# Local attention scores: from VectorE products to TensorE strips that pass through DRAM

## The chip, the core and the metric

The program runs on one core of a Trainium2 chip. The core has a matrix engine (TensorE, PE in the profile, with its weight loads shown apart as PEld), VectorE (DVE), ScalarE (ACT), GpSimd (POOL), and SyncE (SP), whose only work here is to issue DMAs. The engines run side by side, each takes its own instructions strictly in order, and they wait for each other by semaphores. The metric is the device time of one execution in microseconds; lower is better.

## The reference

Eight batches, eight heads, 576 positions, 64 values per head. Two attentions are added, and the sum goes through a maxout layer and an output layer:

```
q_d, k_d, v_d = mean of 4 neighbouring positions (576 -> 144)
out_up    = repeat(softmax(q_d k_d^T / 8) v_d, 4)          # pooled attention
mask      = |row - column| < 4                             # 7 keys per row
out_local = softmax(where(mask, q k^T / 8, -1e9)) v        # local attention
x = (out_up + out_local) as [4608 tokens, 512]
h = max(x w1, x w2, x w3)                                  # 512 -> 768, three times
y = h w_out                                                # 768 -> 512
```

All inputs are float32 (the weights arrive as 64-bit floats and are split on the device). Local attention needs, for each position, seven scores, those of the keys from three before it to three after it.

## The kernel before

**Blocks and groups.** The tokens are cut into nine blocks of 512: block j (0 to 7) holds the first 512 positions of batch j, and block 8 the last 64 positions of all batches. A group n is half a block's heads: block j has the groups 2j and 2j+1, of four heads each (`HH`). For every block, attention makes `x`, `transposes` turns it into the high and low halves `xhi` and `xlo` (a float32 product is made of three fast ones), `mlp_in` runs 216 matmuls of 128x128 by 512 columns, and `mlp_out` 72 more. In the profile these are the lines `pm<-xhi_0r,whi_0r` and so on, and `pm<-wo_1r,hh_0r`; "MLP matmul" below means one of them.

**Dense groups.** The groups 0 to 3 (`DENSE`) do local attention on TensorE: `band_load` loads q and k with positions on partitions (in pieces of 256 B), `band_transposes` turns them with 16 TensorE transposes and ACT copies (plus two small ones for the halo), `band_scores` makes 128x134 strips of scores, whose useful part is a band of seven, and `band_values` multiplies the softmaxed strips with v.

**Sparse groups.** The groups 4 to 17 make their seven scores on VectorE. In `scores(n)`, each of the four heads has q with four neighbouring positions per partition and k with a halo; one multiplication gives `prod` (7 offsets x 256 values per partition), and one reduction gives `s` (28 scores). The softmax runs on `s` for the four heads at once. `values(n)` multiplies v by the seven probabilities, one instruction group per offset, on ACT (four instructions) or POOL (one), and adds them up on DVE into `x`.

**Pooled attention.** `halves` adds neighbours of q, k and v (tiles `hqk`, `qd`, `kd`, `hv`, `vd`), TensorE transposes the pooled q and k into `qkT`, and `tail_pooled` does the last 16 pooled rows apart (tiles `traw`, `th`, `tq`, two more TensorE transposes). `pooled_scores` and `pooled_values` then work on `qkT` (tiles `pd`, `pdt`, `ptl`, `ptd`, `pt`, `ptt`).

**PSUM.** Two sets of four banks: `pm` for the MLP and `pa` for attention.

**What sets the order.** No engine order is written by hand. A `Recorder` records every operation with a priority, the engines that may run it, and the buffers it needs; `place` then goes through the operations as a list scheduler with a table of assumed durations (`price`), chooses engine and buffer, and fixes each engine's order before the program is built. An operation of which two engines are capable goes to the one that would end first. All instructions are issued from one line (L348 before the change, L374 after), so the profile's groups are told apart by their tile names, not by lines. Tiles that share a buffer carry the buffer's name: `pv` also holds the dense groups' q and k, `whi` and `wlo` the dense groups' strips, `y` and `wo` parts of the dense groups' values.

The heart of `scores(n)` before:

```
prod = new([P, NO, FAC * D], tag="prod", name=f"prod_{n}_{g}")
dve.tensor_tensor(out=prod, in0=window(kt, 0, NO), in1=qt.unsqueeze(1).broadcast_to([P, NO, FAC * D]), op=ALU.mult)
dve.tensor_reduce(out=s[:, g], in_=prod.rearrange("p o (f d) -> p o f d", d=D), axis=AX.X, op=ALU.add)
```

Of the kernel before, what the change touches and what calls it, by code (L numbers as in the profile page):

```python
# [10 lines left out]
F32 = mybir.dt.float32  # L11
# [22 lines left out]
SEG = FAC * P  # L34
DENSE = (0, 1, 2, 3)
# [4 lines left out]
def shape_constants():  # L40
    ident = np.eye(P, dtype=np.float32)
    o = np.arange(NO)[:, None] - 3
    f = np.arange(FAC)[None, :]
    mask = np.full((2, P, NO, FAC), 3.0e38, np.float32)
    mask[0, 0][(f + o) < 0] = -8.0e9
    mask[1, TAIL - 1 :: TAIL][:, (f + o) >= FAC] = -8.0e9
    diag = (np.arange(HH * TAIL)[:, None] // TAIL == np.arange(HH)[None, :]).astype(np.float32)
    mask = np.ascontiguousarray(np.stack([mask[0][:, :3], mask[1][:, 4:]])).reshape(2, P, 3 * FAC)
# [3 lines left out]
    return ident, mask, diag, np.ascontiguousarray(band.astype(np.float32))  # L52


ENGINES = ("PE", "DVE", "ACT", "POOL", "SP")
DONE_NS = {"PE": 230.0, "DVE": 150.0, "ACT": 190.0, "POOL": 200.0}
BIAS = {"PE": 0.0, "DVE": 0.0, "ACT": 0.0, "POOL": 0.0}
# [19 lines left out]
class Recorder:  # L77
# [6 lines left out]
    def __init__(self, nc, tc, sb, psum):  # L84
        self.nc, self.tc, self.pools = nc, tc, {"SB": sb, "PSUM": psum}
# [5 lines left out]
    def tile(self, shape, dtype, tag=None, bufs=1, name=None, space="SB"):  # L91
# [6 lines left out]
        info = {"tag": key, "k": len(order[1]), "acc": [], "ops": [], "psum": space == "PSUM", "name": name, "words": int(np.prod(shape[1:])), "dtype": dtype}  # L98
# [4 lines left out]
    def region(self, ap):  # L103
        info = self.of.get(ap.tensor.name)
        if info is None:
            return None
        dims = [tuple(d) for d in list(ap.ap)]
# [14 lines left out]
    def add(self, forms):  # L122

        o = Op()
        o.forms = forms
# [37 lines left out]
    def price(self, eng, method, args, kw):  # L163
# [7 lines left out]
        if eng == "PE":  # L171
            if method == "transpose":
                return max(75.0, 0.86 * n), False
            if args[1].dtype == F32R:
                return 231.0, False
            return 2.0 * max(64.0, 0.86 * n), False
# [20 lines left out]
    def place(self):  # L197
# [43 lines left out]
        while len(out) < len(ops):  # L241
# [17 lines left out]
            if len(o.forms) > 1:  # L259
                ends = []  # L260
                for a in o.forms:
                    c, lock = o.cost[a]
                    ends.append((max(free[a], o.ready, port if lock else 0.0) + c + BIAS[a], a))
# [9 lines left out]
            if e == "SP":  # L273
# [3 lines left out]
                ap = next(a for a in (o.forms[e][0][1][:2]) if a.tensor.name in self.of)  # L277
                other = next(a for a in (o.forms[e][0][1][:2]) if a.tensor.name not in self.of)
                size = list(ap.ap)[0][1] * elems(ap) * 4
                rate = 330.0 if list(other.ap)[-1][1] >= 256 else 180.0  # L280
# [41 lines left out]
    def emit(self):  # L322
# [5 lines left out]
        def real(a):  # L328
# [5 lines left out]
            slot = (space, tag, info["slot"], kind)  # L334
            if slot not in store:
# [24 lines left out]
def local_global_attention_maxout_kernel(ctx: ExitStack, tc: tile.TileContext, q, k, v, w1, w2, w3, w_out, ident_d, mask_d, diag_d, band_d, out):  # L360
# [3 lines left out]
    rec = Recorder(nc, tc, sb, psm)  # L364
# [29 lines left out]
    mask = new([P, 2, 3 * FAC], name="mask")  # L394
# [5 lines left out]
    KW = SEG + 6  # L400
    KB = 2 * FAC * (P + 6)
    band = [new([P, 2 * KW + 2 * (P + 6)], tag=f"w{x}{NFT - 1}", name=f"bandqk_{x}") for x in ("hi", "lo")]
    bandmask = band[0][:, 2 * KW :].rearrange("p (u x) -> p u x", u=2)
# [34 lines left out]
    def load_constants():  # L438
# [3 lines left out]
        sp.dma_start(mask, mask_d.rearrange("m p x -> p m x"))  # L442
        sp.dma_start(diag, diag_d)
        sp.dma_start(bandmask, band_d)
        for pr in range(2):
            dve.memset(band[pr][:, SEG : SEG + 3], 0.0)
# [41 lines left out]

    def tail_pooled(n):
        j, h0 = n // 2, HH * (n % 2)  # L490
        st = state[n]
        tq = st["tq"] = new([N64, 2, 2, D], tag="tq", name=f"tq_{n}")
        for g, src in enumerate((q, k, v)):
            raw = new([N64, FAC * D], tag="traw", name=f"traw_{n}_{g}")
            sp.dma_start(raw, dram(src, ((j * H + h0) * S + FAC * P) * D, [[S * D, HH], [FAC * D, TAIL], [1, FAC * D]]))
            h = new([N64, 2 * D], tag="th", name=f"th_{n}_{g}")
            halves(n, "t", raw, h)
            if g < 2:
                tt(tq[:, g], h[:, :D].unsqueeze(1).broadcast_to([N64, 2, D]), h[:, D:].unsqueeze(1).broadcast_to([N64, 2, D]), ALU.add)
            else:  # L500
                vt = st["vt"] = new([N64, HH, D], tag="vt", name=f"vt_{n}", bufs=2)
                vs = new([N64, D], tag="vs", name=f"vs_{n}")
                tt(vs, h[:, :D], h[:, D:], ALU.add)
                tt(vt, vs.unsqueeze(1).broadcast_to([N64, HH, D]), diag.unsqueeze(2).broadcast_to([N64, HH, D]), ALU.mult)

    def pooled_scores(n):
        st = state[n]
        tq, qkT = st["tq"], st["qkT"]
        qt = qtail[n % 2]
        pst = bank([P, 2, 2, 2, TAIL], "pa", f"pstail_{n}")  # L510
        for i in range(2):
            pe.transpose(pst[:, i], tq[:, i], ident[:N64, :N64])
        for i in range(2):
            pp = slice(64 * i, 64 * i + 64)
            act.copy(qt[pp, :, i], pst[pp, 0, :, i])
            act.copy(qkT[pp, 1, :, P:], pst[pp, 1, :, i])
# [64 lines left out]
    def scores(n):  # L581
        j, h0 = n // 2, HH * (n % 2)
        st = state.setdefault(n, {})
        s = st["p"] = new([P, HH, NO, FAC], tag="s", bufs=2, name=f"s_{n}")
        if j < B:
            hs = {w: new([P, HH, 2 * D], tag="hqk", bufs=2, name=f"h{w}_{n}") for w in "qk"}
            ds = {w: new([P, HH, D], tag=f"{w}d", name=f"{w}d_{n}") for w in "qk"}
        for g in range(HH):
            h = h0 + g
            qt = new([P, FAC * D], tag="q", bufs=2, name=f"q_{n}_{g}")  # L590
            kt = new([P, HW], tag="k", bufs=2, name=f"k_{n}_{g}")
# [5 lines left out]
            if j < B:  # L597
                halves(n, "q", qt, hs["q"][:, g])
                halves(n, "k", kt[:, 3 * D : 7 * D], hs["k"][:, g])
        if j < B:  # L600
            for w in "qk":
                tt(ds[w], hs[w][:, :, :D], hs[w][:, :, D:], ALU.add)
        e0 = 0 if j < B else 4 * FAC
        sf = s.rearrange("p g o f -> p g (o f)")[:, :, e0 : e0 + 3 * FAC]
        dve.tensor_tensor(out=sf, in0=sf, in1=mask[:, j // B].unsqueeze(1).broadcast_to([P, HH, 3 * FAC]), op=ALU.min)
        mx = new([P, HH, FAC], tag="mx", bufs=2, name=f"mx_{n}")
        dve.tensor_reduce(out=mx, in_=s.rearrange("p g o f -> p g f o"), axis=AX.X, op=ALU.max)
        dve.tensor_tensor(out=s, in0=s, in1=mx.unsqueeze(2).broadcast_to([P, HH, NO, FAC]), op=ALU.subtract)
        act.activation(s, s, AF.Exp, scale=0.125)
        z = new([P, HH, FAC], tag="z", bufs=2, name=f"z_{n}")  # L610
        dve.tensor_reduce(out=z, in_=s.rearrange("p g o f -> p g f o"), axis=AX.X, op=ALU.add)
        dve.tensor_scalar_add(z, z, EPS)
        dve.reciprocal(z, z)
        dve.tensor_tensor(out=s, in0=s, in1=z.unsqueeze(2).broadcast_to([P, HH, NO, FAC]), op=ALU.mult)
        if j < B:
            qkT = st["qkT"] = new([P, 2, 2, SD], tag="qkT", name=f"qkT_{n}")
            ps = bank([P, 2, 2, P], "pa", f"psqk_{n}")
            for i, w in enumerate("qk"):
                for pr in range(2):
                    pe.transpose(ps[:, i, pr], ds[w][:, 2 * pr : 2 * pr + 2, :], ident)  # L620
            copy(qkT[:, :, :, :P], ps)

    def values(n):
# [7 lines left out]
        for g in range(HH):  # L631
# [6 lines left out]
            for o in range(NO):  # L638
                muls = [("activation", (pv[:, o, f], vv[:, (o + f) * D : (o + f + 1) * D], AF.Copy), dict(scale=p[:, g, o, f : f + 1])) for f in range(FAC)]
                kw = dict(out=pv[:, o : o + 1], in0=window(vv, o, 1).rearrange("p o (f d) -> p o f d", d=D), in1=p[:, g, o : o + 1].unsqueeze(3).broadcast_to([P, 1, FAC, D]), op=ALU.mult)  # L640
                rec.add({"ACT": muls, "POOL": [("tensor_tensor", (), kw)]})
# [11 lines left out]
    def band_load(n):  # L653
        j, h0 = n // 2, HH * (n % 2)
        st = state.setdefault(n, {})
        q4 = st["q4"] = new([P, FAC, HH, D], tag="pv", bufs=2, name=f"q4_{n}")
        k4 = st["k4"] = new([P, FAC, HH, D], tag="pv", bufs=2, name=f"k4_{n}")
        kh = st["kh"] = new([3, HH, D], tag="qd", name=f"kh_{n}")
        base = (j * H + h0) * S * D
        for t, src in ((q4, q), (k4, k)):  # L660
            for u in range(FAC):
# [242 lines left out]
```

## Time and profile before

| | |
|---|---|
| runs (three) | 861.69, 864.99, 870.87 us; median 864.99 us |
| profiled execution, first to last instruction | 867.8 us |
| busy: PE, PEld, DVE, ACT, POOL | 92%, 71%, 84%, 53%, 31% of that span |
| granted TensorE clock, mean | 0.945 |

The profiled execution's time is known as its span alone; it lies between the second and the third run, 2.8 us above the median. A busy PE is not a PE at its peak, because matmuls overlap and their ends are modelled: whether PE could take more is read from the distance between the starts of matmuls, and from a stretch in which nothing else runs. Idle time of an engine that is not the bottleneck costs nothing.

### The profile page before, as it was taken

What the parts mean: (1) busy time and instruction counts of PE and PEld (TensorE: products, weight loads), DVE (VectorE), ACT (ScalarE), POOL (GpSimd) and SP (SyncE); (2) the same over time, 40 slices, a digit from 0 to 9 for tenths busy, and PEclk for the clock granted to TensorE, in tenths of its full rate; (3) what the DMA queues carried; (4) which work ended last, traced back from release to release, by engine and by line L of the source; (5) the groups of instructions that cost most, each with busy time, mean ns of one, the idle gap of its engine ahead of it and who ended that gap; (6) DMA issues with size and microseconds to landing.
All of it is one profiled execution on the core that took longest, in us unless ns stands there. A gap on an engine that the chain in (4) does not pass through costs nothing.

```text
span 867.8 us, 12330 instructions
## 1 busy us (share of the span) xinstructions
PE 794.8 (92%) x3992; PEld 612.3 (71%) x3992; DVE 727.2 (84%) x1201; ACT 461.5 (53%) x1607; POOL 269.3 (31%) x345
## 2 busy tenths in 40 slices
PE   3779996898999999998989899988999999999997
PEld 3557775686777777676767677766777777788885
DVE  3889959699999999999999999999999999851220
ACT  3656646442738484756466564557564848721111
POOL 0011200003346364334354444444443623500000
PEclk9555998689999999999999999999999999999999
DMA  6844304233323323332223221432232233101002
GB/s 182 228 123 132 95 21 143 77 110 116 100 74 97 116 81 96 100 97 81 88 86 119 88 83 59 158 92 76 80 125 77 74 106 115 35 1 49 1 1 48
DMA packets 71675, 78.71 MB, mean 91 GB/s; under 512 B 30108, under 2 KB 51930, under 8 KB 71610
## 3 DMA queue, kind: packets, MB, share of 16 engines
q1 hardware_dynamic: 71610, 77.93, 29.5%
q8 instruction: 31, 0.51, 0.2%
q14 instruction: 34, 0.28, 0.1%
HBM read 68.47 MB, written 9.44 MB: 90 GB/s over the span
## 4 chain that ended last, share of the span: by engine, by line
DVE 53%; PE 30%; issue 8%; ACT 6%; DMA 1%; SPq 1%; POOL 1%; DVEq 0%; ACTq 0%; POOLq 0%
PE pm L348 23%; DVE pv L348 9%; DVE prod L348 8%; DVE s L348 7%; DVE t L348 7%; PE pa L348 6%; ACT pv L348 4%; DVE wo L348 3%; DVE xlo_0r L348 2%; DVE nm L348 2%; DVE hh_0r L348 1%; DVE x L348 1%; DVE mxb L348 1%; DVE hh_1r L348 1%; DMA v<-in_v_dram 1%
## 5 line engine op out<-in xcount | busy, mean ns | idle before, releaser
L348 PE MATMUL pm<-xlo_0r,whi_0r 128*128 128x512 f32 x648 | 259.7, 401 | 0.0
L348 PE MATMUL pm<-xhi_0r,whi_0r 128*128 128x512 f32 x648 | 259.1, 401 | 0.0
L348 PE MATMUL pm<-xhi_0r,wlo_0r 128*128 128x512 f32 x648 | 258.6, 399 | 0.0
L348 ACT ACTIVATE pv<-v,s 128x64 f32<-128x64 f32 x840 | 210.7, 340 | 28.6 <-DVE s L348 16.7
L348 POOL TENSOR_TENSOR pv<-v,s 128x256 f32<-128x256 f32 x182 | 140.1, 799 | 148.4 <-DVE x L348 64.3
L348 PEld LDWEIGHTS pm<-xhi_0r,wlo_0r 128*128 128x128 f32 x648 | 123.3, 190 | 27.9 <-issue 0.9
L348 PEld LDWEIGHTS pm<-xhi_0r,whi_0r 128*128 128x128 f32 x648 | 123.2, 190 | 28.0 <-issue 0.7
L348 PEld LDWEIGHTS pm<-xlo_0r,whi_0r 128*128 128x128 f32 x648 | 123.1, 190 | 28.0 <-issue 0.7
L348 DVE TENSOR_TENSOR t<-pm,t 128x512 f32<-128x512 f32 x108 | 73.7, 683 | 71.8 <-PE pm L348 70.9
L348 DVE TENSOR_TENSOR prod<-k,q 128x1792 f32<-128x1792 f32 x56 | 117.5, 2098 | 0.2
L348 DVE TENSOR_REDUCE s<-prod 128x28 f32<-128x1792 f32 x56 | 112.4, 2007 | 0.5
L348 DVE TENSOR_TENSOR pv<-pv 128x768 f32<-128x768 f32 x112 | 102.5, 915 | 2.1
L348 PE MATMUL pm<-wo_1r,hh_0r 128*128 128x512 f32 x216 | 87.2, 405 | 4.0 <-ACT wo_1r L348 2.4
L348 PE MATMUL pm<-wo_1r,hh_1r 128*128 128x512 f32 x216 | 86.8, 404 | 0.1
L348 ACT COPY y<-pm 128x512 f32<-128x512 f32 x43 | 24.9, 585 | 57.9 <-PE pm L348 57.4
L348 ACT CAST hh_0r<-t 128x512 fp32r<-128x512 f32 x30 | 18.6, 618 | 67.6 <-DVE t L348 67.6
L348 PEld LDWEIGHTS pm<-wo_1r,hh_0r 128*128 128x128 f32 x216 | 41.1, 190 | 15.0 <-ACT wo_1r L348 3.1
L348 POOL TENSOR_TENSOR th<-traw 64x128 f32<-64x128 f32 x26 | 24.1, 927 | 82.4 <-DMA traw<-in_k_dram 36.2
L348 ACT COPY t<-pm 128x512 f32<-128x512 f32 x54 | 31.3, 581 | 32.8 <-PE pm L348 32.6
L348 PEld LDWEIGHTS pm<-wo_1r,hh_1r 128*128 128x128 f32 x216 | 41.0, 190 | 10.1 <-ACT hh_1r L348 0.5
L348 PE MATMUL pm<-wo_0r,hh_0r 128*128 128x512 f32 x120 | 46.0, 394 | 0.0
L348 PE MATMUL pm<-wo_0r,hh_1r 128*128 128x512 f32 x96 | 38.5, 402 | 0.0
(184 smaller groups left out, 1088.5 us busy)
## 6 DMA issues: line engine op xcount, KB each, us to landing
v<-in_v_dram SPq DMA_DIRECT2D x55, 320.0 KB
k<-in_k_dram SPq DMA_DIRECT2D x55, 320.0 KB
out_dram<-y SPq DMA_DIRECT2D x36, 256.0 KB
q<-in_q_dram SPq DMA_DIRECT2D x56, 128.0 KB
hh<-in_moe_w_dram SPq DMA_DIRECT2D x12, 512.0 KB
pv<-in_moe_w_dram SPq DMA_DIRECT2D x6, 512.0 KB
pv<-in_moe_w_out_dram SPq DMA_DIRECT2D x6, 512.0 KB
pv<-in_q_dram SPq DMA_DIRECT2D x16, 128.0 KB
```

The source lines that it names most:

```text
L348: getattr(self.engines[o.eng], method)(*map(real, args), **{k: real(x) for k, x in kw.items()})
```

## The change

The sparse groups' scores move to TensorE, and all groups get q and k already transposed.

- The program's inputs become `qt` and `kt` (two heads x 64 values on partitions, positions along the row; `kt` padded by three positions on each side), with `qe` and `ke` for block 8. They are prepared outside the device program. `load_qk(n)` loads two tiles of q and two of k per group with rows of 2304 to 2328 B; `band_transposes`, the loads of the halo and the loads of pooled tails of q and k are gone.
- `scores(n)` makes, for each pair of heads, 16 matmuls of 64 positions by 70 keys (strips in which seven of 70 are useful) into two `pa` banks, copies the banks to `sm`, writes `sm` to a DRAM buffer `scr` (four DMAs of 64 x 8 pieces of 280 B per group), and reads it back with a row pitch one element longer, so that the diagonal band lands as seven neighbours (one DMA of 2048 pieces of 28 B per group). The softmax on `s` is as before, with its axes in another order.
- `pooled_qk(n)` adds neighbours directly on the transposed tiles (`hp`, then `qkT`), so that the pooled transposes go.
- `begin(n + 1)` (loads, scores, pooling of the next group) is recorded ahead of `values(n)`, with a priority 100 behind that of group n.
- In the scheduler: prices for small matmuls, for DMAs with short pieces, and DVE as a third choice for the multiplications of `values`, with 3000 ns added against it.

```
+    def load_qk(n):
...
+                t = new([P, width], tag=f"{w}T", bufs=3, name=f"{w}T_{n}_{pr}")
+                if j < B:
+                    sp.dma_start(t, src[j, c0 + pr])
...
+    def pooled_qk(n):
...
+                t = st[w][pr][:, 3 * a : 3 * a + S].rearrange("p (r f) -> p r f", f=FAC)
+                h = new([P, SD, 2], tag="hp", name=f"hp_{n}_{pr}_{a}")
+                pair = [("tensor_tensor", (), dict(out=h, in0=t[:, :, :2], in1=t[:, :, 2:], op=ALU.add)), ("tensor_tensor", (), dict(out=qkT[:, a, pr], in0=h[:, :, 0], in1=h[:, :, 1], op=ALU.add))]
+                rec.add({"POOL": pair, "DVE": pair})
...
     def scores(n):
-            sp.dma_start(qt, row_tokens(q, j, h, 0, FAC * D))
-            load_halo(kt, k, j, h)
-            prod = new([P, NO, FAC * D], tag="prod", name=f"prod_{n}_{g}")
-            dve.tensor_tensor(out=prod, in0=window(kt, 0, NO), in1=qt.unsqueeze(1).broadcast_to([P, NO, FAC * D]), op=ALU.mult)
-            dve.tensor_reduce(out=s[:, g], in_=prod.rearrange("p o (f d) -> p o f d", d=D), axis=AX.X, op=ALU.add)
+        scr = rec.tile([SCR], F32, "scr", 2, f"scr_{n}", "DRAM")
+        for pr in range(2):
+            sps = [bank([P, FAC, KWIN], "pa", f"sb_{n}_{pr}_{i}") for i in range(2)]
+            for t in range(SEG // QT):
+                u, h = divmod(t, 2)
+                for i in range(2):
+                    pp = slice(64 * i, 64 * i + 64)
+                    pe.matmul(sps[i][QT * h : QT * h + QT, u], st["q"][pr][pp, QT * t : QT * t + QT], st["k"][pr][pp, step * t : step * t + KWIN], start=True, stop=True, tile_position=(64 * i, QT * h))
+            sm = new([P, 2, FAC, KWIN], tag="sm", bufs=2, name=f"sm_{n}_{pr}")
+            for i in range(2):
+                copy(sm[:, i], sps[i])
+            for h in range(2):
+                to = (2 * pr * SEG + h * QT) * (KWIN + 1)
+                sp.dma_start(dram(scr, to, [[KWIN, QT], [P * (KWIN + 1), 2 * FAC], [1, KWIN]]), sm[QT * h : QT * h + QT].rearrange("p g u x -> p (g u) x"))
+        s = st["p"] = new([P, FAC, HH, NO], tag="s", bufs=2, name=f"s_{n}")
+        sp.dma_start(s, dram(scr, 0, [[FAC * (KWIN + 1), P], [KWIN + 1, FAC], [SEG * (KWIN + 1), HH], [1, NO]]))
...
     def values(n):
-                rec.add({"ACT": muls, "POOL": [("tensor_tensor", (), kw)]})
+                rec.add({"ACT": muls, "POOL": [("tensor_tensor", (), kw)], "DVE": [("tensor_tensor", (), kw)]}, MUL_BIAS)
...
-    def band_transposes(n, tag):
...
+    def begin(n):
+        load_qk(n)
+        scores(n)
+        if n // 2 < B:
+            pooled_qk(n)
...
     def attention(n):
-        scores(n)
         if j < B:
             tail_pooled(n)
             pooled_scores(n)
+        if n < 2 * B + 1:
+            with at(100.0 * n + 100.0, LAG):
+                begin(n + 1)
         values(n)
```

The order that the scheduler makes of it, at two places. First TensorE in a middle block, where before the change the pooled q and k of a group are turned. `pa` and `pm` are PSUM banks, `ident` the identity matrix, `qd` and `kd` the pooled q and k, `tq` the pooled tails; rows with `xhi` or `xlo` are MLP matmuls. Before:

```order
L348 MATMUL pa_282<-ident_65,qd_92 128x128 x2
L348 MATMUL pa_308<-ident_65,tq_132 128x64 x2
...
L348 MATMUL pm_118<-xhi_0r,wlo_0r 128x512
L348 MATMUL pa_282<-ident_65,kd_1761 128x128 x2
L348 MATMUL pm_118<-xlo_0r,whi_0r 128x512
...
L348 MATMUL pa_144<-qkT_150 128x144
```

After the change the same engine in a middle block, right behind the transposes of the pooled probabilities (`pd`, `pdt`, `ptl`, `ptd`); `kT` and `qT` are the transposed inputs:

```order
L374 MATMUL pa_136<-ident_67,pd_276 128x128 x4
L374 MATMUL pa_138<-ident_67,pdt_302 128x64
L374 MATMUL pa_138<-ident_67,ptl_338 64x128
L374 MATMUL pa_138<-ident_67,ptd_341 64x64
L374 MATMUL pa_376<-kT_111,qT_105 64x70
L374 MATMUL pa_130<-kT_111,qT_105 64x70
...
L374 MATMUL pm_119<-wo_1r,hh_0r 128x512
L374 MATMUL pm_119<-wo_1r,hh_1r 128x512
L374 MATMUL pm_119<-wo_0r,hh_0r 128x512
L374 MATMUL pa_136<-kT_85,qT_81 64x70 x4
L374 MATMUL pa_138<-kT_85,qT_81 64x70 x4
```

What moved: the three insertions of pooled transposes are gone; the next group's 32 score matmuls stand in two runs of 16, with three MLP matmuls between them, and the second run takes the two banks that the transposes ahead of it filled.

Second SP's queue in a middle block. Before, q and k come per head (`q`, `k`), with v and the pooled tails (`traw`):

```order
L348 DMA q_148<-in_q_dram 128x256
L348 DMA k_104<-in_k_dram 128x640
L348 DMA out_dram<-y_276 128x512
L348 DMA q_154<-in_q_dram 128x256
L348 DMA k_280<-in_k_dram 128x640
L348 DMA v_96<-in_v_dram 128x640
```

After, per group the loads of `qT` and `kT`, four writes to `scr` and the readback into `s`:

```order
L374 DMA scr_1435<-sm_121 64x8x70
L374 DMA s_1911<-scr_1759 128x16x7
L374 DMA kT_87<-in_kt_dram 128x582
L374 DMA scr_1435<-sm_121 64x8x70
L374 DMA scr_1435<-sm_252 64x8x70 x2
L374 DMA v_91<-in_v_dram 128x640
L374 DMA s_1564<-scr_1435 128x16x7
L374 DMA v_93<-in_v_dram 128x640
```

What moved: the readback stands in the same queue as the loads of v, and behind the writes that it must wait for.

More of the change, by code (lines that the diff above doesn't have):

```diff
@@ L34 @@
 SEG = FAC * P
+QT = 64
+KWIN = QT + NO - 1
+SCR = HH * SEG * (KWIN + 1)
 DENSE = (0, 1, 2, 3)
@@ L276, in place @@
                 free[e] = t + c
-                ap = next(a for a in (o.forms[e][0][1][:2]) if a.tensor.name in self.of)
-                other = next(a for a in (o.forms[e][0][1][:2]) if a.tensor.name not in self.of)
+                two = o.forms[e][0][1][:2]
+                ap = next(a for a in two if self.of.get(a.tensor.name, {"tag": "-"})["tag"][0] == "SB")
+                other = next(a for a in two if a is not ap)
                 size = list(ap.ap)[0][1] * elems(ap) * 4
-                rate = 330.0 if list(other.ap)[-1][1] >= 256 else 180.0
+                run = list(other.ap)[-1][1]
+                rate = 330.0 if run >= 256 else 180.0 if run >= 32 else 40.0
                 dma_free = max(dma_free, t + 1200.0) + size / rate
@@ L334, in real @@
             slot = (space, tag, info["slot"], kind)
+            if space == "DRAM":
+                if slot not in store:
+                    store[slot] = self.pools[space].tile([width], kind, tag=f"{tag}_{info['slot']}", name=f"{tag}_{info['slot']}")
+                base = store[slot]
+                return bass.AP(tensor=base.tensor, offset=base.offset + a.offset, ap=[list(d) for d in a.ap])
             if slot not in store:
@@ L393, in local_global_attention_maxout_kernel @@
     ident = new([P, P], name="ident")
-    mask = new([P, 2, 3 * FAC], name="mask")
+    mask = new([P, 2, FAC, 3], name="mask")
     diag = new([N64, HH], name="diag")
@@ L399, in local_global_attention_maxout_kernel @@
     zd = new([P, 5], name="zd")
[L400 removed]
     KB = 2 * FAC * (P + 6)
[L402 to L403 removed]
+    bandmask = new([P, 2, P + 6], tag=f"whi{NFT - 1}", name="bandmask")
     prob = [new([P, KB + 2 * FAC * 32], tag=f"w{x}{NFT - 2}", name=f"bandp_{x}") for x in ("hi", "lo")]
@@ L487, in halves @@
         tt(dst, src[..., : 2 * D], src[..., 2 * D :], ALU.add, engines)
+    def load_qk(n):
+        j, c0 = n // 2, 2 * (n % 2)
+        st = state.setdefault(n, {})
+        for w, width, src, end in (("q", S, qt_d, qe_d), ("k", S + 6, kt_d, ke_d)):
+            st[w] = []
+            for pr in range(2):
+                t = new([P, width], tag=f"{w}T", bufs=3, name=f"{w}T_{n}_{pr}")
+                if j < B:
+                    sp.dma_start(t, src[j, c0 + pr])
+                else:
+                    t = t[:, : end.shape[2]]
+                    sp.dma_start(t, end[c0 + pr])
+                st[w].append(t)
+    def pooled_qk(n):
+        st = state[n]
+        qkT = st["qkT"] = new([P, 2, 2, SD], tag="qkT", name=f"qkT_{n}")
+        for a, w in enumerate("qk"):
+            for pr in range(2):
+                t = st[w][pr][:, 3 * a : 3 * a + S].rearrange("p (r f) -> p r f", f=FAC)
[4 more added lines that the diff above has]
+            pp = slice(64 * i, 64 * i + 64)
+            copy(qtail[n % 2][pp, :, i], qkT[pp, 0, :, P:])
     def tail_pooled(n):
@@ L491, in tail_pooled @@
         st = state[n]
[L492 to L504, printed above, removed]
+        raw = new([N64, FAC * D], tag="traw", name=f"traw_{n}")
+        sp.dma_start(raw, dram(v, ((j * H + h0) * S + FAC * P) * D, [[S * D, HH], [FAC * D, TAIL], [1, FAC * D]]))
+        h = new([N64, 2 * D], tag="th", name=f"th_{n}")
+        halves(n, "t", raw, h)
+        vt = st["vt"] = new([N64, HH, D], tag="vt", name=f"vt_{n}", bufs=2)
+        vs = new([N64, D], tag="vs", name=f"vs_{n}")
+        tt(vs, h[:, :D], h[:, D:], ALU.add)
+        tt(vt, vs.unsqueeze(1).broadcast_to([N64, HH, D]), diag.unsqueeze(2).broadcast_to([N64, HH, D]), ALU.mult)
     def pooled_scores(n):
         st = state[n]
[L508 to L516, printed above, removed]
+        qkT, qt = st["qkT"], qtail[n % 2]
         sps = [bank([P, 2, SD], "pa", f"s{i}_{n}") for i in range(2)]
@@ L600, in scores @@
[L600 to L607, printed above, removed]
@@ L615, in scores @@
[L615 to L621, printed above, removed]
+        dve.tensor_tensor(out=s, in0=s, in1=z.unsqueeze(3).broadcast_to([P, FAC, HH, NO]), op=ALU.mult)
     def values(n):
@@ L850, in block @@
                 attention(n)
+        if 2 * j + 1 == DENSE[-1]:
+            with at(100.0 * n + 100.0, LAG):
+                begin(n + 1)
     def turn(j):
@@ L889 @@
     arrays, args = {}, []
-    named = [(name, inputs[name]) for name in _INS] + list(zip(("ident", "mask", "diag", "band"), shape_constants()))
+    named = list(zip(("qt", "kt", "qe", "ke"), transposed(inputs["q"], inputs["k"])))
+    named += [(name, inputs[name]) for name in _INS] + list(zip(("ident", "mask", "diag", "band"), shape_constants()))
     for name, a in named:
```

109 lines of the change are left out of this document (46 added, 63 removed).

## The prediction

> **What bounds the kernel now.** I read the page's busy shares and slices first. Column by column, DVE stands at nine tenths or more from the ninth slice to the thirty-fourth, and PE reads eight or nine over the same stretch and on to the end.
>
> ```profile
> PE   3779996898999999998989899988999999999997
> DVE  3889959699999999999999999999999999851220
> PEclk9555998689999999999999999999999999999999
> ```
>
> Two engines that both look full need a closer view, since a busy PE is not a PE at its peak. So I cut the span where the MLP takes over (74.6), where sparse groups begin (205) and where attention ends (763), and asked for all engines, and then for the instructions on the `pm` banks alone.
>
> ```profile
> 74.60:205.00 130.40, 118.63 (x708) 90.27 (x707) 106.38 (x234) 64.20 (x191) 12.04 (x13) 0.86 0.29 88
> 205.00:763.00 558.00, 528.36 (x2540) 405.28 (x2541) 543.95 (x776) 338.73 (x1249) 252.24 (x319) 0.99 0.29 93
> 763.00:862.00 99.00, 99.00 (x430) 80.36 (x429) 22.20 (x33) 16.52 (x28) 0.00 (x0) 1.00 0.06 19
> 205.00:763.00 558.00, 461.75 (x1888) 350.72 (x1889) 54.47 (x80) 39.22 (x68) 0.99 0.29 93
> 763.00:862.00 99.00, 99.00 (x429) 80.36 (x429) 11.06 (x16) 8.81 (x15) 1.00 0.06 19
> ```
>
> Columns: length, then busy time and count of PE, PEld, DVE, ACT, POOL (absent where nothing ran), clock, DMA share, GB/s. The last two rows are the `pm` ones. After 763 nothing but the MLP runs: 429 matmuls in 99.0 us, 0.2308 us each, and this is what one costs when PE waits for nobody. In the middle stage 1888 of them at that price are 435.7 us; 122.3 of 558 us are left for attention's insertions on PE and for waiting. DVE is busy for 544 of the 558. So DVE is the fuller engine, but PE has at most 122 us to give, and most of that is work. How much is waiting, the two views of waits say (the same window, PE's matmuls first, then its weight loads):
>
> ```profile
> PE pa L348 <- DVE pdt L348: 6.4, 4, 2.4
> PE pa L348 <- ACT pd L348: 0.5, 2, 0.3
> PEld pa L348 <- issue: 19.6, 61, 1.2
> PEld pa L348 <- DVE pdt L348: 8.1, 4, 2.8
> PEld pa L348 <- ACT pv L348: 7.8, 7, 2.7
> PEld pa L348 <- DVE t L348: 0.2, 1, 0.2
> ```
>
> The 13 rows of PE, from the first to the last shown, add up to 30.7 us; the 20 rows of weight loads that another engine ended add up to 44.6. A matmul's idle time hides under the modelled end of the one before, so the second is nearer the truth; I take 40 us of waiting and 82 of work.
>
> That DVE is full and yet only some 40 us can be won is the whole argument: **the next bound stands right behind the present one.**
>
> **What goes from DVE.**
>
> ```profile
> L348 DVE TENSOR_TENSOR prod<-k,q 128x1792 f32<-128x1792 f32 x56 | 117.5, 2098 | 0.2
> L348 DVE TENSOR_REDUCE s<-prod 128x28 f32<-128x1792 f32 x56 | 112.4, 2007 | 0.5
> L348 DVE TENSOR_TENSOR hqk<-k 128x128 f32<-128x128 f32 x23 | 7.4, 323 | 0.0
> L348 DVE TENSOR_TENSOR hqk<-q 128x128 f32<-128x128 f32 x22 | 6.7, 305 | 0.0
> L348 DVE TENSOR_TENSOR q<-whi 128x256 f32<-128x256 f32 x8 | 3.6, 448 | 0.0
> L348 DVE TENSOR_TENSOR qkT<-q 128x128 f32<-128x128 f32 x16 | 5.1, 320 | 0.5
> L348 DVE COPY pt<-pa 128x512 f32<-128x512 f32 x6 | 4.1, 680 | 0.9 <-PE pa L348 0.9
> ```
>
> The products and reductions are 229.9 us, the pooled halves on DVE 14.1. Added on DVE: 48 pairs `hp` and `qkT` in sparse groups, scaled from the rows for 256 and 128 elements to 288 and 144, 0.50 + 0.36 us, together 41; 30 of the 56 copies `sm` (the rest stand on ACT) at 280/512 of 0.68, 11. DVE's middle stage falls from 544 to about 352 us, and no engine but PE stays near its limit: ACT loses 100 of 840 multiplications to POOL, which had 252 us of work in 558. I cost all this at nothing, since PE's 500 us of work in the stage covers it; without that cover it would be paid at the rows' prices.
>
> **What is added on PE.** No row shows a 64x64 tile with 70 columns. The nearest is the dense strip: eight matmuls in two row halves (each recorded twice, as float32 is made in two passes), between MLP matmuls.
>
> ```profile
> 87.82 0.40 PE L348 MATMUL pm<-xlo_0r,whi_0r 128*128 128x512 f32 x1
> 88.14 1.19 PE L348 MATMUL pa<-whi 64*128 64x134 f32 x16
> 89.27 0.50 PE L348 MATMUL pm<-xhi_0r,whi_0r 128*128 128x512 f32 x1
> 89.60 0.39 PE L348 MATMUL pm<-xhi_0r,wlo_0r 128*128 128x512 f32 x1
> ```
>
> From 87.82 to 89.60 is 1.78 us; less two MLP matmuls, the insertion costs 1.32. Its 16 records leave in eight steps of two, (89.27 - 88.14)/8 = 0.14 us a step with the way in and out, some 0.115 without. The new run has 16 matmuls, 32 records; at 70/134 of the columns a step is 0.060 us. Two side by side: 16 x 0.060 + 0.4 for the switches = 1.4. Four side by side (its tiles lie in four quarters): 0.9. None: 32 x 0.060 + 0.4 = 2.3. As half the runs follow other attention work and share its switch, I take 1.2 us, ends 0.9 and 2.3. There are 28 runs, 24 of them in the middle stage: **+29 us** (22 to 55).
>
> The Trainium skill, "TensorEngine Tiling (Array Packing)", section Key Properties, says that different tiles work in parallel, and that a change of tiling mode drains the engine. The strip's steps of two agree with the first; four at once is shown by no run here. By that page the run would be 0.9 us, and the sum 7 us lower.
>
> **What goes from PE.**
>
> ```profile
> L348 PE MATMUL pa<-ident,tq 64*128 64x64 f32 x32 | 7.9, 272 | 4.2 <-POOL tq L348 3.0 <-DVE tq L348 1.3
> L348 PE MATMUL pa<-ident,qd 128*128 128x128 f32 x24 | 4.8, 280 | 1.9 <-DVE qd L348 1.8
> L348 PE MATMUL pa<-ident,kd 128*128 128x128 f32 x24 | 4.7, 277 | 1.5 <-DVE kd L348 1.5
> L348 PE MATMUL pm<-ident,pv 128*128 128x128 f32 x32 | 7.6, 426 | 0.0
> L348 PE MATMUL pa<-ident,pv 128*128 128x128 f32 x32 | 5.5, 332 | 0.0
> ```
>
> In the middle stage `qd` and `kd` (9.5 us) and 24 of 32 `tq` (5.9): **-15 us**. Of the 40 us of waits, most are ended by DVE or by ACT behind DVE. With DVE at two thirds I leave 12 and take **-28 us**; ends -40 (none left) and -15 (the static order still makes PE wait, now for evictions of the new strips).
>
> **Before 205 us.** Here the dense groups set the pace, and the chain of that window is spread: `pm` and `pa` on PE hold 39% of it.
>
> ```profile
> by line: PE pm L348 24.5%; PE pa L348 14.9%; DVE wo L348 10.4%; DVE mxb L348 5.0%; DVE t L348 4.1%; SPq L348 3.5%; DVE wlo L348 3.5%; DMA v<-in_v_dram 3.3%; DVE y L348 3.2%; DVE whi L348 2.9%; DVE wlo_0r L348 2.8%; issue 2.7%; DVE q L348 2.
> 9.72 0.34 PE L348 MATMUL pm<-ident,qd 3*128 3x3 f32 x2 [9.72 <-DMA qd<-in_k_dram]
> 13.60 1.70 PE L348 MATMUL pm<-whi 64*128 64x134 f32 x16
> ```
>
> The 64 transposes of dense q and k (13.1 us in the rows above) and eight `tq` (2.0) go; at 40 to 50% on the chain that is 6 to 7 us. The first strip starts at 13.60, after nine DMAs of small pieces and 16 transposes; with four loads and no transposes it can start some 5 us earlier. Against it stand four score runs, 5 us, and DVE's weight splits, which no edit touches. **-7 us**, ends -25 (all of PE's relief and the earlier start pass through) and +4.
>
> **DMAs and the wait that is added.** Per group there are 2048 pieces of 280 B out and 2048 of 28 B back.
>
> ```profile
> q1 hardware_dynamic: 71610, 77.93, 29.5%
> ```
>
> 29.5% of 16 engines' 867.8 us over 71610 packets is 57 ns each, at 1088 B on average. At that price for each of 4096 pieces a group costs 14.6 us of transfer time, at a share by bytes 2 us; against some 40 us per group both fit beside the MLP. The readback waits on SP for four writes to land, and behind it stand loads of v. What covers it: scores of the next group come right after the pooled probabilities, while present values still run (four heads, two buffers of v loaded ahead). I cost it at nothing; ends 0 and +1 us per group, 14.
>
> **The sum.** Against the span: middle stage +29 - 15 - 28 = -14; before it -7; after it 0, for those matmuls stay back to back. 867.8 - 21 = 847; the median of the runs lies 2.8 lower, so **844 us**.
>
> **Rivals.**
> - *PE has more room than it seems* (821 us). Weight loads are busy for 405.28 of 558 us in the middle stage, 72.6%, and 81.2% where PE is never idle; by that ratio 59 us of the stage are free or lost to switches. If waits go to zero (-12 more), runs take 0.9 us (-7) and the early stage gives 4 us more, the time is 821. Against it: the rows of waits name 45 us at most. The Trainium skill's page "Trainium Kernel Development and Optimization", Best Practices, says to judge distance to the limit by the weight loads' share and not by matmul busy time; by it this rival gains, and the trace bears it out as far as 81.2% is the ceiling here.
> - *The strips do not overlap* (874 us). At 2.3 us a run, 24 runs cost 55 us, 26 more than in the sum, and four early ones 4 more: 844 + 30 = 874. For it: only two tiles are seen at once, in one direction. The gain is then used up. Each 0.1 us per run is worth 2.8 us, so the zero lies near 1.95 us.
> - *PE waits for its banks* (886 us): slower. The second run of 16 takes the banks that the pooled transposes filled, and these come free after three copies on ACT, which stand behind multiplications of `values`. PE has waited for ACT's `pv` before, up to 2.7 us. If each of 28 runs waits 1.5 us, 42 us are added. From 0.75 us a run on, nothing is won; from 1.1 us on, it is slower by over 1%. Against it: ACT has more idle time than before.
> - *The readback is late*: values of each group wait for `s`. At 4 us for each of 14 groups it would be 56 us (900 us), but only once the lead of a whole group is used up. Little speaks for it.
>
> **How the numbers follow.** Chances: forecast 0.56, more room 0.22, no overlap 0.11, banks 0.08, readback 0.03. The runs before spread over 1%, and less than 1% (856.3 to 873.6) can't be told from no change. The forecast's own range is 828 to 860; the range of 8 in 10 takes in more room and no overlap: 814 to 876. Faster by over 1%: more room and 0.48 of the forecast's 0.56, 0.70. Within 1%: the rest of it and half of no overlap, 0.14. Slower: the other half, banks and readback, 0.16.
>
> **What would show it.** DVE busy near two thirds in the middle stage, `prod` gone, and PE never idle for long: MLP matmuls at 0.23 us and blocks of some 83 us. A run of 16 strips between 0.9 and 1.5 us. First strip before 10 us. I am wrong if PE's waits stay above 30 us, if a strip run takes over 2 us, or if PE's rows name `sm` or `pt` copies as what ended its waits.

## The result, and the profile after

The changed kernel takes 842.13 us (median of 4 runs, 841.72 to 843.63), against 864.91 for the kernel before (4 runs, 861.69 to 870.87): a ratio of 0.973, 95% interval 0.969 to 0.977. The prediction was 844, with a range of 814 to 876. The profiled execution took 841.72 us, its span is 839.9 us, 27.9 less than before. The medians lie only 22.8 us apart, so some 5 us of what is read below from one execution of each kernel may be scatter.

The busy tenths and the clock of the page of the kernel after, in the same 40 slices, and the chain by engine, before and then after:

```profile
PE   3969986999999999999999999999999999999997
DVE  6898979478787767764776388547844772540220
PEclk9559987589999999999999999999999999999999
DVE 53%; PE 30%; issue 8%; ACT 6%; DMA 1%; SPq 1%; POOL 1%; DVEq 0%; ACTq 0%; POOLq 0%
PE 87%; DVE 9%; ACT 1%; DMA 1%; SPq 1%; issue 1%; DVEq 0%; ACTq 0%
```

VectorE is no longer full in any slice but a few early ones, and PE reads nine from the eighth slice to the last but one. The chain, which ran through DVE for 53% before, runs through PE for 87%. To see where the time went, I cut both traces at the same events: the first matmul of the second block's MLP (210.3 before, 206.7 after), that of the eighth (725.0 and 700.4), and the last one. The windows view, two rows of before and then two of after (length, then busy time and count of PE, PEld, DVE, ACT, POOL, then clock, DMA share, GB/s):

```profile
210.30:725.00 514.70, 487.81 (x2365) 372.91 (x2365) 505.43 (x730) 310.74 (x1148) 235.82 (x300) 1.00 0.30 96
725.00:862.00 137.00, 135.20 (x593) 109.37 (x591) 55.48 (x77) 43.16 (x127) 12.10 (x16) 1.00 0.10 30
```

```profile
206.70:700.40 493.70, 493.50 (x3089) 385.97 (x3082) 331.23 (x692) 281.30 (x1009) 146.30 (x200) 1.00 0.36 94
700.40:833.90 133.50, 133.50 (x585) 108.69 (x583) 40.66 (x64) 34.24 (x89) 10.64 (x15) 1.00 0.07 21
```

The six blocks in the middle take 21.0 us less, the rest 3.5 less, the start 3.6 less: 28.1, and with 0.2 more behind the last matmul the difference of the spans, 27.9. In the middle DVE went from 505 of 515 us to 331 of 494, and PE is busy in 493.5 of 493.7. The waits of the changed kernel between 205 and 751 us, all rows of PE and the first of its weight loads:

```profile
PE pa L374 <- DVE t L374: 0.2, 1, 0.2
PEld pa L374 <- issue: 13.1, 53, 0.4
PEld pa L374 <- ACT sm L374: 3.3, 9, 0.4
PEld pm L374 <- issue: 2.5, 11, 0.2
PEld pa L374 <- DVE t L374: 1.8, 4, 0.6
```

Of 30.7 us of waits on PE, 0.2 are left. No row of PE names `pt` or `sm`; both ended waits of weight loads, of at most 0.4 us each.

The score runs themselves, in the timeline of PE (start, duration, engine, operation, tiles, count), beside the transposes of the pooled probabilities and alone between MLP matmuls:

```profile
468.43 0.24 PE L374 MATMUL pa<-ident,ptd 64*64 64x64 f32 x1
468.60 0.72 PE L374 MATMUL pa<-kT,qT 64*64 64x70 f32 x32
469.25 0.50 PE L374 MATMUL pm<-xlo_0r,whi_0r 128*128 128x512 f32 x1
...
469.81 0.40 PE L374 MATMUL pm<-xhi_0r,wlo_0r 128*128 128x512 f32 x1
470.14 0.73 PE L374 MATMUL pa<-kT,qT 64*64 64x70 f32 x32
470.80 0.50 PE L374 MATMUL pm<-xlo_0r,whi_0r 128*128 128x512 f32 x1
471.14 0.40 PE L374 MATMUL pm<-xhi_0r,whi_0r 128*128 128x512 f32 x1
```

From 468.60 to 469.25 a run takes 0.65 us where other attention work has already paid for the switch; alone it costs 471.14 - 469.81 less two MLP matmuls, 0.87. I had taken 1.2. Inside a run the 32 records start in eight groups of four, 7 ns apart, and the groups come every 0.061 us: four tiles at once.

### The profile page after: what moved, and what is told of

Its sections match the earlier page's. It is cut to its first block, busy times and chain, and to the rows that moved or that the text cites. A ratio compares the mean times of both kernels' runs of the same rounds, so it can differ in the third digit from the quotient of the medians.

```text
span 839.9 us, 13435 instructions
## 1 busy us (share of the span) xinstructions
PE 797.0 (95%) x4736; PEld 619.5 (74%) x4736; DVE 537.7 (64%) x1163; ACT 420.6 (50%) x1433; POOL 171.8 (20%) x243
## 4 chain that ended last, share of the span: by engine, by line
PE 87%; DVE 9%; ACT 1%; DMA 1%; SPq 1%; issue 1%; DVEq 0%; ACTq 0%
PE pm L374 71%; PE pa L374 16%; DVE wo L374 2%; DVE y L374 1%; DMA hh<-in_moe_w_dram 1%; DVE t L374 1%; SPq L374 1%; DVE wlo L374 1%; DVE hh_1r L374 1%; DVE mxb L374 1%; DVE hp L374 0%; DVE xlo_0r L374 0%; DVE nm L374 0%; ACT wlo L374 0%; ACT whi L374 0%
## 5 line engine op out<-in xcount | busy, mean ns | idle before, releaser
L374 POOL TENSOR_TENSOR pv<-v,s 128x256 f32<-128x256 f32 x207 | 152.1, 767 | 410.5 <-DVE s L374 196.7
L374 ACT ACTIVATE pv<-v,s 128x64 f32<-128x64 f32 x740 | 186.2, 338 | 17.8 <-issue 7.8
L374 PE MATMUL pm<-wo_0r,hh_0r 128*128 128x512 f32 x120 | 47.7, 399 | 1.1 <-DVE wo_0r L374 1.0
L374 PEld LDWEIGHTS pa<-kT,qT 64*64 64x64 f32 (+1 forms) x960 | 28.1, 142 | 10.5 <-ACT sm L374 3.3
L374 PE MATMUL pa<-kT,qT 64*64 64x70 f32 (+1 forms) x960 | 35.7, 239 | 0.0
L374 ACT CAST hh_1r<-t 128x512 fp32r<-128x512 f32 x24 | 14.8, 616 | 36.5 <-DVE t L374 36.5
```

The lines of the kernel that those rows point to most:

```text
L374: getattr(self.engines[o.eng], method)(*map(real, args), **{k: real(x) for k, x in kw.items()})
```

## The experiments

Each kernel is the changed one with the edit shown, except the dense part alone, which starts from the kernel before. "Second block" is the start of its MLP, "six blocks" the time from there to the eighth block's, "VectorE" its busy time in that stretch, all from the profiled execution; the median is of all runs of a kernel, and the ratio is to the kernel before as it ran beside it (medians of 864.4 to 865.6 us).

| kernel | median us | ratio to before, interval | second block | six blocks | VectorE |
|---|---|---|---|---|---|
| before | 864.91 | 1 | 210.3 | 514.7 | 505 |
| after | 842.13 | 0.973 (0.969 to 0.977) | 206.7 | 493.7 | 331 |
| scores by one quarter | 859.83 | 0.993 (0.991 to 0.995) | 210.2 | 510.5 | 333 |
| scores by two quarters | 851.57 | 0.983 (0.978 to 0.989) | 206.4 | 504.3 | 329 |
| scores twice | 850.41 | 0.983 (0.978 to 0.988) | 205.0 | 503.7 | 329 |
| one free reduction | 844.95 | 0.976 (0.971 to 0.981) | 196.1 | 502.0 | 408 |
| two free reductions | 849.72 | 0.983 (0.979 to 0.987) | 211.0 | 495.8 | 460 |
| three free reductions | 901.93 | 1.041 (1.034 to 1.047) | 211.2 | 528.7 | 515 |
| reductions in the chain | 879.41 | 1.015 (1.010 to 1.020) | 208.3 | 528.3 | 478 |
| no lead | 918.39 | 1.063 (1.059 to 1.067) | 202.5 | 570.0 | 314 |
| readback twice | 838.49 | 0.970 (0.966 to 0.973) | 206.6 | 491.6 | 332 |
| dense part alone | 855.65 | 0.989 (0.983 to 0.995) | 193.9 | 519.9 | 510 |
| longer prices, lag 300 | 850.25 | 0.981 (0.976 to 0.986) | 211.4 | 495.6 | 339 |
| longer prices | 864.64 | 0.999 (0.996 to 1.002) | 225.7 | 496.8 | 327 |

Two theories stood against each other on PE's side: PE is the bound after the change, and a score run costs what its side-by-side tiles leave (the tiles are the four 64x64 quarters of PE's 128x128 array, chosen by `tile_position`); or PE still has room.

**Scores by one quarter.**

```
-            for t in range(SEG // QT):
-                u, h = divmod(t, 2)
-                for i in range(2):
+            for i in range(2):
+                for t in (0, 2, 4, 6, 1, 3, 5, 7):
+                    u, h = divmod(t, 2)
```

> The same 16 matmuls of a score run, written quarter by quarter: four of one 64x64 tile position in a row, then four of the next, so that side-by-side work is left only where the quarter changes. Theory (four tiles work at once because neighbours in the order lie in four different quarters, and PE is the bound): a run is then 32 records one after the other at the 0.061 us that the trace of the changed kernel shows between groups of four, 1.95 us plus 0.3 for the way in and out, against 0.65 to 0.87 now; 1.5 us more in each of some 25 runs that stand on the path, 37 us: 842 becomes 879 (868 to 886). Rival A (the run's price is the change of tiling, not the matmuls): 842, at most 846. Rival B (PE still has slack under its busy rows): below 855.

Measured: 859.83, and 16.8 us more in the six blocks. The timeline of PE in that kernel:

```profile
479.75 1.60 PE L374 MATMUL pa<-kT,qT 64*64 64x70 f32 x32
481.27 0.50 PE L374 MATMUL pm<-xhi_0r,wlo_0r 128*128 128x512 f32 x1
```

A run beside the transposes takes 1.52 us instead of 0.65. Rivals A and B fall. The loss is half of what I expected, since the records still went off in pairs at many places (steps of 5 and 56 ns in turn), so this was never one tile at a time.

**Scores by two quarters.** The same loops with `t` in the order 0, 2, 4, 6, 1, 3, 5, 7 and `i` inside.

> The same 16 matmuls, ordered so that only two different tile positions (the two row halves, one column half) alternate, as in the dense strips of the kernel before; the column half changes once. Theory (side by side by quarters): 16 steps of 0.061 us instead of 8, 0.5 us more per run, 25 runs on the path: 842 becomes 854 (850 to 858), about a third of what the order by single quarters costs. Rival (the row halves alone give the overlap): same as the changed kernel, 842 +- 3.

Measured: 851.57, 10.6 us more in the six blocks, as the theory had it.

```profile
473.49 1.01 PE L374 MATMUL pa<-kT,qT 64*64 64x70 f32 x32
474.43 0.50 PE L374 MATMUL pm<-xlo_0r,whi_0r 128*128 128x512 f32 x1
```

0.94 us a run, against 0.65. The same work costs 0.65, 0.94 or 1.52 us by its order alone, and it reaches the end: priced as above, the insertions between MLP matmuls of the six blocks grew by 17 us with one quarter and by 11 with two, and the blocks by 16.8 and 10.6. Overlap by quarters is shown, and PE as the bound too.

**Scores twice.** `for _ in range(2):` around the matmul.

> Each score matmul is issued twice in a row into the same place (the second writes the same values). Nothing else is added. The second copy follows in the same quarter, so two neighbours no longer lie side by side and a run is up to 64 records. Theory (PE is the bound after the change and every us on it shows in the time): between 8 more steps of 0.061 us (0.5 us per run, 854) if the copies still overlap with the other quarters, and 2.3 us per run (900) if they do not; likeliest that only every second pair overlaps, 1.2 us more per run, 25 runs, 872. The sign is the test: clearly slower. Rival (PE has 20 us of room by the share of its weight loads): below 850.

Measured: 850.41, 10.0 us more in the six blocks, less than expected. Two runs in a row show why:

```profile
467.28 2.44 PE L374 MATMUL pa<-kT,qT 64*64 64x70 f32 x128
469.65 0.50 PE L374 MATMUL pm<-xlo_0r,whi_0r 128*128 128x512 f32 x1
```

1.18 us per doubled run: the copies still overlapped with other quarters. The median is only 0.4 us above the rival's 850, but the stage speaks against it: 10.0 us more there, for 25 runs of which each is some 0.5 us longer.

On VectorE's side the question was whether its relief brought the gain, and how much of it was needed.

**One free reduction per head.**

```
+            for _ in range(1):
+                dve.tensor_reduce(out=junk, in_=window(vv, 0, NO)..., axis=AX.X, op=ALU.add)
             pv = new([P, NO, FAC, D], tag="pv", bufs=2, name=f"pv_{n}_{g}")
```

> Adds one VectorE reduction of 128x1792 elements (2.0 us in the trace of the kernel before) per head of the sparse groups, read from the head's v tile into a tile that nothing uses: 56 x 2.0 = 112 us of VectorE work, half of what the change took from it; its busy time in the middle stage goes from about two thirds to about 85%. Theory (VectorE is off the bound and its relief beyond PE's limit is unused): 842 to 848. Rival (the gain is proportional to VectorE's relief): half of 22.8 us comes back, 853 or more.

Measured: 844.95, the theory's. By stages it is less clean: the six blocks took 8.3 us more, and the second block started 10.6 us earlier; PE waited 6.7 us in those blocks, in seven places and for five tiles. So the median agrees with the theory, but a gain at the start that has nothing to do with the edit hides a loss behind it; this run alone shows nothing of VectorE's slack.

**Two free reductions per head** (`range(2)`).

> Adds two such VectorE reductions per head (56 x 4.0 = 225 us), as much as products and reductions took before the change; their results go into a tile that nothing uses. VectorE's work is then 763 us against 727 before the change, and in the middle stage 354 + 205 = 559 us where the stage lasts 539. Theory (the time fell because VectorE fell under PE's limit): VectorE is the bound again, its middle stage is at least 559 us plus stalls, and the time goes back to 865 or more, 870 to 900. Rival (the time fell because transposes left PE, not because of VectorE): below 850.

Measured: 849.72; the theory's number is wrong by 20 us. The windows view of the six blocks says why:

```profile
210.97:706.80 495.83, 494.06 (x3080) 385.60 (x3075) 460.38 (x669) 286.01 (x1031) 183.62 (x278) 1.00 0.33 91
```

VectorE did not reach 559 us. The lines view of VectorE for the same stretch shows what was added there:

```profile
L374 DVE TENSOR_REDUCE junk<-v 128x28 f32<-128x1792 f32 x97 | 195.0, 2010 | 3.0 <-DMA v<-in_v_dram 2.3
```

195 us were added, yet its busy time rose by 129, and GpSimd's by 37: the planner moved other work away. At 460 of 496 us, 93%, PE lost 2.1 us. So that much load need not cost anything. It is not free in every order, though: the kernel with one reduction lost 8.3 us at 408 of 502 us, 81%. And this run could not tell whether load or something else had bound the kernel before. Two more runs did.

**Three free reductions per head** (`range(3)`).

> Three of the VectorE reductions per head instead of two, results unused. With two, VectorE was busy for 460 of the 496 us between the starts of the second and the eighth block, because the planner gave part of its other work to GpSimd, and PE did not wait. A third adds 97 x 2.0 = 195/2 = 97 us there: 557 us. Theory (a stage lasts as long as the fuller of PE, 494 us, and VectorE): 557 us plus stalls, some 63 us more, less what GpSimd still takes over (20 to 30 us): 842 becomes 885 (870 to 910). Rival (what counted before the change was not VectorE's load but that values waited for its products): load without users costs little, below 860.

```profile
211.20:739.90 528.70, 505.67 (x3062) 394.49 (x3058) 515.24 (x662) 279.67 (x992) 189.26 (x298) 0.97 0.31 83
PE pa L374 <- POOL vd L374: 8.5, 3, 4.1
PE pa L374 <- DVE t L374: 6.6, 3, 3.7
```

Measured: 901.93. VectorE is busy for 515 of 529 us, 97%, PE waits again, and 20 us more are lost behind the eighth block's start, where 25 of the 168 reductions were left over (50 us). The stage follows the fuller engine, as the theory said. (The reductions also hold the tiles of v, and SP's queue waited 236.5 us for them there; but VectorE itself stood idle for only 13 of 529 us, so its load set the pace.)

**Reductions in the chain.**

```
         sp.dma_start(s, dram(scr, 0, ...))
+        mx = new([P, FAC, HH], tag="mx", bufs=2, name=f"mx_{n}")
+        for g in range(HH):
+            t = st["k"][g // 2]
+            for _ in range(2):
+                dve.tensor_reduce(out=mx, in_=bass.AP(..., ap=[t.ap[0], [64, FAC], [32, HH], [1, 112]]), axis=AX.X, op=ALU.add)
```

> The same amount of VectorE work as with two reductions per head (112 reductions of 128x1792 elements, 225 us), but placed where products and reductions stood: eight per group, read from the transposed k and written into the tile of the maxima, which the group's softmax then overwrites. So the multiplications of values wait for them. Theory (only the load counts): as with two free reductions per head, 850 (845 to 856). Rival (the place in the chain counts: 16 us per group ahead of the softmax): values start late, PE waits again, 862 or more.

```profile
208.30:736.60 528.30, 512.01 (x3113) 393.29 (x3114) 478.45 (x721) 305.61 (x1089) 163.35 (x232) 0.98 0.32 86
PE pa L374 <- DVE vd L374: 3.7, 2, 3.3
PE pa L374 <- DVE pdt L374: 2.7, 2, 2.0
```

Measured: 879.41, the rival's. The 225 us that cost 2 us in these blocks as free work (195 of them fell there) cost 35 ahead of the softmax (207 fell there), with VectorE at 91%. PE waits once more for VectorE's `pdt`, which headed its waits before the change. So the place counts beside the load, and the kernel before had both: 98% load, and products that values waited for. (The reductions also delay loads: in these blocks SP's queue waited 1.0 us for them, and 20.5 us for `hp` on VectorE, 0.9 in the changed kernel. How much of the 35 us comes that way and how much through the softmax was not tried apart.)

**No lead.** `begin(n)` at the start of `attention(n)`, in place of `begin(n + 1)` ahead of `values(n)`.

> The loads, scores and pooled sums of a group are recorded at the start of its own attention, not ahead of the values of the group before; all operations are the same. The attention banks are handed out in the order of recording, so scores of the next group then stand behind the present group's pooled values and the turn. Theory (the lead hides copies, writes, readback and softmax, some 10 us or more per group, in which the multiplications of values have nothing to do): 14 groups x 4 to 7 us, 842 becomes 900 to 940 if nothing else covers it. Rival (VectorE and ACT have so much room now that the order of recording does not matter): 842 to 850.

```profile
202.50:772.50 570.00, 508.92 (x3027) 400.76 (x3026) 314.24 (x651) 279.87 (x990) 135.41 (x181) 0.93 0.29 76
PE pa L374 <- DVE vd L374: 61.1, 5, 16.3
```

One of the five places, in the timelines of SP, DVE and ACT:

```profile
439.17 0.61 SPq L374 DMA_DIRECT2D s<-scr  x1
442.99 0.21 DVE L374 TENSOR_TENSOR s<-s,mask 128x48 f32<-128x48 f32 x1 [8.32 <-DMA s<-scr]
451.15 12.51 ACT L374 ACTIVATE pv<-v,s 128x64 f32<-128x64 f32 x52
```

Measured: 918.39, slower than before the change. The same operations, the least VectorE time of all, and PE waits 61.1 us in five places for `vd`, the pooled v that the values make; PE runs in order, so the MLP stands behind. The six blocks take 76 us more than in the changed kernel: 61 are these waits, and PE is busy for 15 more, at a granted clock of 0.93 instead of 1.00. In the place shown, SP issues the last write to `scr` at about 428 us and the readback only at 439.17, behind a write of output that waits for ACT's `y`; the softmax ends at 448.4, ACT's multiplications of values run until 463.7, and PE goes on at 463.35. So without the lead the scores, their way through DRAM, the softmax and the values stand one behind the other on the path. What the way through DRAM costs alone was not measured.

**Readback twice.** The DMA into `s` issued a second time.

> The readback of 2048 pieces of 28 B is issued twice per group into the same tile, the second behind the first. Theory (the readback lies under the lead of a group and DMA has room): 842 +- 3. Rival (the readback is on the path): 14 times the time of one readback, 4 us or more each, 898; or, if only its queue time counts, 14 x 0.6 = 8 us, 850.

Measured: 838.49, six blocks 491.6 us: nothing lost. The two intervals against before overlap (0.966 to 0.973 here, 0.969 to 0.977 for the changed kernel), so I do not call it faster. The readback is hidden.

**Dense part alone**, in the kernel before: `qT` and `kT` of the dense groups by DMA from transposed copies, without `band_transposes`' transposes and copies; sparse groups as they were.

> The kernel before with one part of the change alone: the four dense groups load transposed q and k instead of transposing on PE; sparse groups keep their products and reductions on VectorE. The change as a whole brought the start of the second block's MLP from 210.3 to 206.7 us and the span from 867.8 to 839.9. Theory (the middle stage carries the gain): the start of block 1 some 3 us earlier, nothing further on, 865 becomes 862 (858 to 866). Rival (a good part of the gain is the dense groups' work and the earlier start): 850 or less.

```profile
60.00:193.90 133.90, 120.29 (x684) 90.11 (x684) 115.37 (x258) 61.56 (x185) 15.28 (x14) 0.89 0.30 93
193.90:713.80 519.90, 496.39 (x2365) 380.07 (x2365) 510.09 (x731) 311.07 (x1149) 234.89 (x302) 0.98 0.30 95
```

Measured: 855.65, between theory and rival. The start gained 16.4 us, and the middle, with VectorE at 510 of 520 us, gave 5.2 back. The dense part is worth some 9 us by itself, more than I allowed, though how much of its start is the scatter described below stays open; without the scores' move VectorE stays full and the middle gains nothing.

**Planner's prices.** Both add 90, 100 and 200 ns to every assumed duration on VectorE, ScalarE and GpSimd; the first also lowers `LAG` to 300.

> The changed kernel with the planner's assumed durations raised towards the trace (VectorE +90 ns, ScalarE +100 ns, GpSimd +200 ns an instruction; 128x512 on VectorE is then 0.69 us as in the rows) and its lag between engines lowered from 600 to 300 ns. The operations are the same, only order and choice of engine change. Theory (in the middle stage PE waits for nobody, so only the stage before the second block can gain; over the experiments its end lay between 194 and 211 us whatever was edited): 842 becomes 832 to 842. Rival (nothing left to order): 842 +- 2. If the middle stage gets waits again it is slower.

> The raised durations alone, with the lag left at 600 ns. Theory: the start of the second block moves by up to 10 us either way and the middle stage stays at some 494 us: 832 to 850. Rival: as the changed kernel, 842 +- 2.

Measured: 850.25 and 864.64. The middle stage is 496 and 497 us, no shorter than the changed kernel's 494. The start moved, but the wrong way: 211.4 and 225.7 instead of 206.7. Prices nearer the trace gave no better order, and no version here beats the changed kernel beyond doubt.

## Why the prediction was right, point by point

**What bounded the kernel.** Right in its main sentence: VectorE full, PE right behind. Load is shown as one cause (three free reductions), the place in the chain as another (reductions in the chain); the prediction spoke of the first only.

**VectorE at two thirds, costed at nothing.** Right: 331 of 494 us, 67%, and PE's waits were gone. In one order 93% cost PE 2 us, in another 81% cost 8.

**Score runs +29.** Too high, the mis-sized term. 25 runs fell into the six blocks. By their insertions (11 beside the transposes at 0.66, 4 in longer ones at about 0.8, 6 alone at 0.87 to 1.02, 4 cut in two halves at 0.84 each) they cost some 23 us, 0.9 each. I had doubted that four tiles run at once. The Trainium skill, "TensorEngine Tiling (Array Packing)", Key Properties, says that different tiles work in parallel; the trace agrees (groups of four, 0.061 us apart), and the 0.9 us a run that the prediction gave beside that page is what came out.

**Removed transposes -15.** A little too high: I added up busy rows, which overlap. As insertions between MLP matmuls `tq` cost 0.4 us, a pair of `kd` or `qd` 0.2; some 14 us in the six blocks.

**A term that I had not seen.** The pooled scores, one insertion of 1.26 us a group before, are now mostly cut in two or more, each with a switch of its own (`qkT` alone 0.9, `qtail` alone 0.57): some 6 us.

**Waits -28.** Right in kind, too low: I kept 12 of 40 us, and hardly any stayed. From the other terms, 21.0 + 23 + 6 - 14 = 36 us of waiting went; insertions of the kernel before were some 32 us above the cheapest of their kind, and gaps between MLP matmuls shrank by 6. No new wait took their place.

**Middle stage.** -14 predicted; measured -21.0, and -24.5 with the last blocks, which the prediction's window reached into up to 763.

**Before 205 us, -7.** Half of it: -3.6. The first strip started at 7.63 us, before 10 as said, and the first block's MLP 12.5 us earlier (62.1 instead of 74.6), but most of that was lost again. Over these kernels the second block starts anywhere from 193.9 to 225.7 us. One cause is shown below, the granted clock; the rest of that scatter is open.

**Readback at nothing.** Right, and shown by the readback issued twice. What covers it is the lead, and to lose that as a whole cost the six blocks 76 us; I had named the cover and not its price.

**Rivals.** Strips without overlap, banks behind ScalarE's copies and a late readback did not occur. Of "more room than it seems" two parts came true (no waits, 0.9 us a run), its 821 us did not: the smaller removal, the cut insertions and the start took back what they gave. Weight loads are busy for 78% of the six blocks (385.97 of 493.7), not 81%, and yet added PE time reached the end in all three score experiments.

The span was 7 us under the predicted 847: runs -6, removed +1, cut insertions +6, waits -8, last blocks -3.5, start +3.4. The median was 2 under. So close a hit is in part luck: misses of 6 and 8 us went both ways, and the profiled execution before lay 2.8 us above its median by its span, the one after 2.2 below.

## What to carry to other kernels

Cut both traces at the same events of the bounding engine, price each insertion as the time between its neighbours less their own, and what is left over is waiting. Before moving work off a full engine, ask how full the next one is, and whether the work's place in the chain or its amount is what hurts: dummy work with and without users tells these apart. Here a detour through DRAM cost nothing while a whole group of other work lay between its two ends, and to take that lead away cost three times what the move had gained.

## What the hardware showed that I had not expected

The same list of PE instructions ran at two speeds before the second block. The windows view of `pa` matmuls on PE, two rows of the changed kernel and then two of the one with one free reduction (length, busy time and count, clock, DMA share, GB/s):

```profile
156.00:161.00 5.00, 5.00 (x33) 0.50 0.00 0
161.00:166.00 5.00, 5.00 (x80) 0.50 0.05 16
```

```profile
152.00:157.00 5.00, 5.00 (x59) 1.00 0.00 0
157.00:162.00 5.00, 4.06 (x92) 1.00 0.37 96
```

The stretch from the first transpose of the pooled probabilities to the next MLP matmul took 13.1 us (153.34 to 166.42) at a granted clock of 0.50 from 154.2 on, and 7.9 us (151.35 to 159.23) at 1.00: 5.2 us by the clock alone. In both a pause of about 2 us on PE stands ahead (1.96 and 2.39). The Trainium skill, "TensorE: Matmul & The Clock Gate", Part 1, says that the array falls to half rate after an idle window and rises after about 3.4 us of sustained work. The half rate agrees with the MLP matmuls at a clock of 0.50, which start every 0.43 us instead of 0.23 (timeline of PE, changed kernel):

```profile
149.43 0.63 PE L374 MATMUL pm<-xhi_0r,wlo_0r 128*128 128x512 f32 x1
149.85 0.63 PE L374 MATMUL pm<-xlo_0r,whi_0r 128*128 128x512 f32 x1
```

The rise does not agree: PE had small attention matmuls back to back for the 10 us of the rows above, at 0.50. Finer windows put the changes of the changed kernel's clock at 150.8 us (up), 154.2 (down) and 174.7 (up), 3.4 us and six times 3.4 us apart; the last rise came after 3.4 us in which only MLP matmuls started. The whole pause of 1.96 us lies in the 3.4 us ahead of the fall. In the other kernel the clock rose at 147.0; steps of 3.4 us from there would cut its pause of 2.39 us at 150.5 into 1.5 and 0.9. That would explain why its clock stayed up, but no run moves the pause against those steps, so it is not shown.
